# FNet mixing gated with a Mish MLP: the fifth block of columns takes its second row from the first row's partial and s3

## The chip, the cores and the metric

The kernel runs on one core of one Trainium2 chip. The core has TensorE (PE, matrix products), VectorE (DVE), ScalarE (ACT), GpSimd (POOL, hardly used here) and SyncE (SP), from which nearly all transfers between the chip's memory (HBM) and the on-chip memory are issued. PE adds its products up in PSUM, eight banks of 128 x 512 floats; DVE and ACT read the banks out. Each engine works off its own instructions in order and waits for the others by semaphores. The metric is the device time of one execution in microseconds (us); what counts is the median of several runs.

## The reference

```python
a = jnp.einsum("bsd,ed->bse", x, dft_hid_re)
b = jnp.einsum("bsd,ed->bse", x, dft_hid_im)
y = jnp.einsum("ts,bse->bte", dft_seq_re, a) - jnp.einsum("ts,bse->bte", dft_seq_im, b)
...
h = jnp.einsum("bsd,df->bsf", x, w1) + b1
act = h * jnp.tanh(softplus(h))          # Mish
mlp = jnp.einsum("bsf,fd->bsd", act, w2)
...
g = _sigmoid((x * gate_w).sum(-1, keepdims=True))
return g * y + (1 - g) * mlp
```

Here x is 2048 x 640 (s by d), the Fourier matrices are 2048 x 2048 and 640 x 640, w1 is 640 x 1728 and w2 1728 x 640, all in float32.

## The kernel before

**Products.** A float32 operand is split into a high and a low part (`split`, line 82): ACT copies it into a tile of the reduced type fp32r (line 80), DVE subtracts that from the original (line 77). A product of two split operands is three matmuls: high by high, high by low, low by high (`mm3`, line 91; all matmuls have line 89). Line 80 is thus every plain ACT copy and line 77 every DVE operation on two tensors.

**Stages.** The sequence transform comes first (four problems sq0 to sq3: real and imaginary matrix, two halves of the times each), then the hidden transform (hd0, hd1), then the first dense layer with Mish (written separately, `dense_rest` and `dense_first`), then the second dense layer (ou0, ou1). Between stages the results go through scratch buffers in HBM: u, y, act. The gate is worked out beside the sequence stage (`gate`, line 885: DVE sums, then two matmuls into a bank of their own, a sigmoid on ACT); g and 1 - g are kept in the buffers g and q. ou0 multiplies its results by q and adds y on the way out; ou1, called "early" in the code, has q already in its operands and adds y to intermediate results.

**A problem.** Each of the eight problems in the sequence, hidden and out stages is a product of 640 columns (five blocks of 128, the stationary operand) with two rows of 512 times, t1 and t2, over kh pairs of k (8, 5 and 6). The moving operands of a pair are a11 and a12 (t1, first and second half of k), a21 and a22 (t2). Four of the five blocks are multiplied with seven products for eight, in the manner of Strassen and Winograd, with sums s1 to s4 of the moving operands. The fifth block is multiplied plainly, into the banks d1 (row t1) and d2 (row t2). A problem is three functions:

- `first`: a11 by two blocks (bank pair a) and by the fifth block (d1);
- `second`: steps "22", "21", "s2" and "s1" for every k. "22" multiplies a22 into p4 and d2, "21" multiplies a21 into d2, "s2" into a, "s1" into b. With the last k of "21", d2 is finished and copied out (`done`), and the kept results are copied back into the banks c;
- `third`: steps "12" (banks c and d1), "s3" (a) and "s4" (b), with s3 = a11 - a21.

For sq1, sq2, hd1 and ou1 `first` runs well before `second`, and its results lie "aside" in HBM (three tiles, `part` 0 to 2); `a_ready` and the code after "21" load them back into banks (`preload`, line 281, an ACT copy into PSUM). In ou0 and ou1 `second` begins with a step `rest` (line 564) for the k that are left over, which opens its banks itself (the flag in its list of uses).

**Order.** Everything is emitted by one loop over the steps (line 1040), and each engine runs its instructions in the order in which this loop emits them. An iteration i first prepares the steps up to i + 7 (LEAD; 6 in the dense stage): sums and splits on DVE and ACT. Loads are issued 9 steps ahead of that, as long as enough of the 20 slots of the pool f are free. Then come the matmuls of step i, the stores that are due (three steps after the result), the step's `post` (reading banks out), the events that `at` registered for i, and then jobs (weights to be prepared, the gate) if an estimate of DVE's clock is behind PE's. PSUM banks and slots are handed out from lists, first freed first given. All loads and stores but one go through SP's queue in this order; one that has to wait for its slot or its value holds up those behind it.

Of the kernel before, what the change touches and what calls it, by code (L numbers as in the profile page):

```python
# [45 lines left out]
def fnet_mish_gate(ctx: ExitStack, tc: tile.TileContext, xn, xt, c_re, c_im, wd_re, wd_im,  # L46
# [134 lines left out]
    def b_sums(f, g):  # L181

        t = FS.get()
        tt(f[:, A2], f[:, B2], f[:, A2], OP.subtract)
        tt(f[:, B2], g[:, B2], f[:, B2], OP.subtract)
        tt(t[:, A2], g[:, B2], f[:, A2], OP.subtract)
        tt(t[:, B2], g[:, A2], t[:, A2], OP.subtract)
        return t
# [104 lines left out]
    class Problem:  # L293
# [8 lines left out]
        def first(self, new=False):  # L302
            st, kh = self.st, self.st.kh
            pa, pd = ("ax", "dx") if self.aside else ("a", "d1")
            for k in range(kh):
# [24 lines left out]
                def post():  # L330
                    if self.aside:
                        for dst, f in zip(self.aside, copy_out(pa) + copy_out(pd)):
                            store(dst, f, f)
                    else:
                        KEEP["p1"] = copy_out("a", True)
                if new:
                    raw += [(("xa", k), st.row(k)[:, A2])]
                if last:
                    takes[len(steps)] = 3 if self.aside else 2
# [3 lines left out]
        def second(self):  # L343
# [4 lines left out]
            def sums(k, raws):  # L348
                a22, a21, a11 = (RAW.pop(r[0]) for r in raws)
                s1 = FS.get()  # L350
                tt(s1, a21, a22, OP.add)
                tt(a11, s1, a11, OP.subtract)
                own.update({("22", k): a22, ("21", k): a21, ("s1", k): s1, ("s2", k): a11})
# [3 lines left out]
                "21": lambda k: [("d2", blocks(st.XA[k], 2 * P, 1))],  # L357
# [3 lines left out]
            opens = {("22", "p4"), ("22", "d2"), ("s1", "b")}  # L361
# [5 lines left out]
            def post(p, k):  # L367
# [4 lines left out]
                elif p == "21":  # L372
                    self.done("d2", 4, t2)
# [7 lines left out]
                    if self.aside:  # L381
                        d = [RAW.pop(("part", 2))]
                        if self.early:
                            y = YT.pop((4, t1))
                            tt(d[0], d[0], y, OP.add)
                            FS.put(y)
                        preload("d1", d)
                        FS.put(*d)
# [16 lines left out]
            if st.kind == "out":  # L405
                def e_post():
                    KEEP["r22"] = add_out("e", ys(t2, 2, 3)) if self.early else copy_out("e")
                if self.early:
                    self.y_load(n - 4, t2, 2, 3)
                rest(t2, [("e", 2, True), ("e", 3, True), ("p4", 0, True), ("p4", 1, True), ("d2", 4, True)], e_post)  # L410
            for p, k in in_turn(kh, ("22", "21", "s2", "s1"), ("22", "21", "s2", "s1"), ("22", "21", "s2", "s1")):
# [7 lines left out]
                def mms(p=p, k=k, key=key):  # L419
                    for name, b in uses[p](k):  # L420
                        product(name, b, key, k == 0 and (p, name) in opens and not (st.kind == "out" and name != "b"),
                                k == kh - 1)
                    op_done(key)
                    if self.end and (p, k) in ends:
                        W.put(st.XA[k])
                        if k == kh - 1:
                            W.put(*[w for w in st.XT2 if w])
                preps.append(lambda p=p, k=k, key=key: c_split(key, own.pop((p, k))))
                step(raw, preps, mms, lambda p=p, k=k: post(p, k))
                if k == kh - 1:  # L430
                    takes[i] = (p == "21" or p == "s1" and 2) if self.early else 1 if p == "21" else 2
                    if self.early and p != "s1":
                        takes[i - 4] = 2
                        if p == "21":
                            self.y_load(i - 4, t2, 4)
                            self.y_load(i - 4, t1, 0, 1, 4)
                        else:
                            self.y_load(i - 4, *{"22": (t2, 0, 1), "s2": (t1, 2, 3)}[p])
                if (p, k) == ("21", kh - 1):
                    done = i  # L440
            if self.out:
                for t in (t1, t2):
                    at(n - 2, lambda t=t: QT.update({t: fs_load(qsc[t])}))
                self.y_load(done - 5, t2, 4)
            ends = {("s1", k) for k in range(kh)}
            if self.aside:
                for j in range(3):
                        at(n - 6 if j < 2 else done - 6, lambda j=j: RAW.update({("part", j): fs_load(self.aside[j])}))
# [3 lines left out]
        def third(self, over=False):  # L452
# [3 lines left out]
            def sums(k, raws):  # L456
                a12, a11, a21, a22 = (RAW.pop(r[0]) for r in raws)
                tt(a11, a11, a21, OP.subtract)
                FS.put(a21)
                tt(a22, a22, a11, OP.subtract)  # L460
                tt(a22, a12, a22, OP.subtract)
                own.update({("12", k): a12, ("s3", k): a11, ("s4", k): a22})
# [3 lines left out]
                "s3": lambda k: [("a", blocks(st.XT13[k], 2 * P, 2))],  # L466
# [13 lines left out]
            def post(p, k):  # L480
# [4 lines left out]
                elif p == "s3":  # L485
# [4 lines left out]
                    free_banks("a")  # L490
                elif p == "12":
# [5 lines left out]
            for p, k in in_turn(kh, ("12", "s3", "s4"), ("12", "s3", "s4"), ("s3", "12", "s4")):  # L497
# [14 lines left out]
                def mms(p=p, k=k, key=key):  # L512
# [4 lines left out]
                    op_done(key)  # L517
                    if self.end and p == "s4":
                        W.put(st.XB[k], st.XT13[k])
                preps.append(lambda p=p, k=k, key=key: c_split(key, own.pop((p, k))))  # L520
                step(raw, preps, mms, lambda p=p, k=k: post(p, k))
                if k == kh - 1 and p != "s3":
                    takes[i] = 3 if p == "12" else 2
                if self.out and k == kh - 1:
                    self.y_load(i - (4 if p == "s3" else 2), *{"s3": (t2, 0, 1, 2, 3), "12": (t1, 0, 1, 4), "s4": (t1, 2, 3)}[p])
# [5 lines left out]
        def done(self, name, d, t):  # L531

            for j, ps in enumerate(PS.pop(name)):
# [4 lines left out]
                elif self.early and name == "d2":  # L538
                    y = YT.pop((d, t))
                    tt(f, ps, y, OP.add)  # L540
                    FS.put(y)
# [591 lines left out]
```

## Time and profile before

| | us |
|---|---|
| median of 3 runs | 886.82 |
| lowest, highest | 885.35, 889.29 |
| span of the profiled execution (what its own time is counted by) | 882.2 |
| PE busy | 864.0 (98%) |
| DVE busy | 724.2 (82%) |
| ACT busy | 477.5 (54%) |
| matmuls | 3780 |
| bytes moved | 217.32 MB |

The span of the profiled execution is from its first to its last instruction; a run's time is somewhat longer, since it holds what lies around them. Busy times are of each engine by itself, and they overlap. In the lists of waits a row names the engine, its line and the tile it writes, what it waited for, the total, the number and the longest. In the windows each engine has its busy time and its number of instructions, and PEclk is the clock that TensorE was granted, 1.00 being full. In the timeline a row is the start, the duration, the engine, the line, the operation and the tiles (written <- read), with the idle time just before it in brackets and what ended that.

### The profile page before, as it was taken

How to read it: one execution, taken by the hardware profiler on the slowest of the kernel's cores; microseconds unless marked ns; L12 is line 12 of the kernel's file. 1: busy time of each engine (PE TensorE's matmuls, PEld its weight loads, DVE VectorE, ACT ScalarE, POOL GpSimd, SP SyncE). 2: the span in 40 equal slices, each digit the busy share in tenths (PEclk: the TensorE clock that was granted, in tenths of full speed). 3: DMA queues.
4: the chain of work that ended last, by engine and by line, in shares of the span. 5: the costliest groups of instructions: out<-in, count | busy, mean ns of one | idle time of the engine just before them, and what ended most of it. 6: DMA issues, size and time to landing. Idle time of an engine off the chain costs nothing.

```text
span 882.2 us, 12203 instructions
## 1 busy us (share of the span) xinstructions
PE 864.0 (98%) x3780; PEld 710.4 (81%) x3780; DVE 724.2 (82%) x1262; ACT 477.5 (54%) x909; POOL 0.2 (0%) x4
## 2 busy tenths in 40 slices
PE   8999999999999999999999999899899999999998
PEld 6888888888888888888888888687688788888886
DVE  5999987899799668998997987663875889798994
ACT  6756545454565545647665667543644656442442
POOL 0000000000000000000000000000000000000000
PEclk9999999999999999999999999999999999999999
DMA  9975759596889664768767795489676777394952
GB/s 323 328 236 175 245 185 324 164 312 235 302 275 351 202 221 156 259 226 283 265 236 273 247 316 178 138 308 367 204 256 214 268 260 240 133 330 142 367 203 107
DMA packets 119392, 217.32 MB, mean 246 GB/s; under 512 B 13600, under 2 KB 16032, under 8 KB 119328
## 3 DMA queue, kind: packets, MB, share of 16 engines
q1 hardware_dynamic: 119184, 216.43, 71.6%
q8 instruction: 29, 0.48, 0.2%
q14 instruction: 35, 0.29, 0.1%
q10 hardware_dynamic: 144, 0.13, 0.0%
HBM read 170.11 MB, written 46.40 MB: 245 GB/s over the span
## 4 chain that ended last, share of the span: by engine, by line
PE 93%; DVE 3%; ACT 1%; DMA 1%; issue 1%; SPq 0%; DVEq 0%; ACTq 0%
PE ps L89 93%; DVE f L77 1%; DVE wl L77 1%; ACT wh L80 1%; DMA y<-f 1%; DVE rl L77 0%; DMA f<-in_xn_dram 0%; ACT f L671 0%; DMA act<-f 0%; DVE fx L77 0%; ACT f L80 0%; ACT rh L80 0%; SPq L1031 0%; SPq L1051 0%; DVE f L477 0%
## 5 line engine op out<-in xcount | busy, mean ns | idle before, releaser
L89 PE MATMUL ps<-rh,wh 128*128 128x512 f32 x1067 | 415.7, 390 | 7.4 <-ACT f L80 3.4
L89 PE MATMUL ps<-rh,wl 128*128 128x512 f32 x1053 | 409.4, 389 | 0.0
L89 PE MATMUL ps<-rl,wh 128*128 128x512 f32 x1052 | 409.1, 389 | 0.0
L80 ACT ACTIVATE rh<-f 128x512 fp32r<-128x512 f32 x413 | 243.7, 624 | 158.3 <-DVE f L77 103.9
L77 DVE TENSOR_TENSOR rl<-f,rh 128x512 fp32r<-128x512 f32 x411 | 267.0, 685 | 47.7 <-ACT rh L80 47.0
L89 PEld LDWEIGHTS ps<-rh,wh 128*128 128x128 f32 x1067 | 200.4, 188 | 52.7 <-ACT f L80 5.0
L89 PEld LDWEIGHTS ps<-rh,wl 128*128 128x128 f32 x1053 | 197.7, 188 | 40.9
L89 PEld LDWEIGHTS ps<-rl,wh 128*128 128x128 f32 x1052 | 197.4, 188 | 40.9 <-DVE rl L77 0.2
L77 DVE TENSOR_TENSOR f<-f,f 128x512 f32<-128x512 f32 x303 | 207.0, 689 | 19.2 <-DMA u<-f 6.3
L80 ACT ACTIVATE f<-ps 128x512 f32<-128x512 f32 (+1 forms) x146 | 84.9, 593 | 92.7 <-PE ps L89 74.7
L80 ACT ACTIVATE wh<-f 128x512 fp32r<-128x512 f32 (+2 forms) x158 | 68.9, 475 | 49.4 <-DVE f L77 40.4
L77 DVE TENSOR_TENSOR f<-ps,f 128x512 f32<-128x512 f32 x90 | 59.0, 685 | 35.1 <-PE ps L89 35.1
L77 DVE TENSOR_TENSOR wl<-f,wh 128x512 fp32r<-128x512 f32 (+2 forms) x157 | 73.8, 502 | 16.2 <-ACT wh L80 16.0
L89 PE MATMUL ps<-wh,wh 128*128 128x512 f32 x201 | 79.3, 395 | 5.4 <-ACT f L80 2.8
L89 PE MATMUL ps<-wl,wh 128*128 128x512 f32 x196 | 77.0, 393 | 0.0
L89 PE MATMUL ps<-wh,wl 128*128 128x512 f32 x195 | 76.6, 393 | 0.0
L77 DVE TENSOR_TENSOR wl<-fx,wh 128x640 fp32r<-128x640 f32 (+3 forms) x82 | 43.7, 554 | 11.6 <-ACT wh L80 11.6
L671 ACT ACTIVATE f<-f,b1s 128x512 f32<-128x512 f32 x36 | 25.9, 721 | 49.2 <-DVE f L77 49.2
L89 PEld LDWEIGHTS ps<-wh,wh 128*128 128x128 f32 x201 | 38.0, 189 | 15.4 <-ACT f L80 4.2
L80 ACT ACTIVATE wh<-fx 128x128 fp32r<-128x128 f32 (+5 forms) x83 | 40.6, 514 | 10.5 <-DMA fx<-in_xn_dram 3.5
L89 PEld LDWEIGHTS ps<-wh,wl 128*128 128x128 f32 x195 | 37.0, 190 | 7.8
L89 PEld LDWEIGHTS ps<-wl,wh 128*128 128x128 f32 x196 | 37.1, 189 | 7.5
(43 smaller groups left out, 177.3 us busy)
## 6 DMA issues: line engine op xcount, KB each, us to landing
f<-in_c_re_dram SPq DMA_DIRECT2D x128, 256.0 KB, 4.2
f<-in_c_im_dram SPq DMA_DIRECT2D x128, 256.0 KB, 4.1
f<-act SPq DMA_DIRECT2D x84, 256.0 KB, 5.2
f<-u SPq DMA_DIRECT2D x80, 256.0 KB, 4.6
f<-in_xt_dram SPq DMA_DIRECT2D x64, 256.0 KB, 4.6
act<-f SPq DMA_DIRECT2D x54, 256.0 KB, 4.5
u<-f SPq DMA_DIRECT2D x40, 256.0 KB, 3.5
y<-f SPq DMA_DIRECT2D x40, 256.0 KB, 4.5
```

The costliest lines, as they stand in the source:

```text
L77: nc.vector.tensor_tensor(o, a, b, op=op)
L80: nc.scalar.activation(o, a, AF.Copy, scale=scale)
L89: nc.tensor.matmul(ps, a, b, start=start, stop=stop, skip_group_check=True)
L671: nc.scalar.activation(o[rows], src[rows], AF.Mish, bias=b1s[rows, f:f + 1])
```

## The change

Row t2 of the fifth block is a21 X1 + a22 X2, where X1 and X2 are the fifth block's stationary parts. Before, both products are made in `second`. After, a21 is written as a11 + s3 with s3 = a21 - a11: the product of a11 with X1 is d1's partial from `first`, s3 X1 is made in `third` in the step "s3", and a22 X2 stays in `second`. So:

- the steps "21" are gone; a21 is not split, and s1 is formed in its slot (one slot of f less). Steps in all: 540 before, 486 after;
- d2 begins with the kept partial. In a problem with its `first` just before, the partial is copied out of d1 and into d2 at the end of `first`; in the others the event `d_ready`, one step before `second` begins, copies it from its tile (in ou1 with y added before on DVE);
- d2 stays open to the end of the last "s3" of `third` and is read out there; all eight banks are then in use in `third`;
- the preloads of c and d1 move from "21" to "22", and the loads of y move with the steps;
- s3 and the stationary sum that goes with it change sign.

DVE operations on two tensors: 1231 before, 1177 after; ACT activations: 907 before, 866 after; matmuls and transfers are as many as before (3780, 829).

```diff
--- before.py
+++ after.py
@@ -182,7 +182,7 @@
 
         t = FS.get()
         tt(f[:, A2], f[:, B2], f[:, A2], OP.subtract)
-        tt(f[:, B2], g[:, B2], f[:, B2], OP.subtract)
+        tt(f[:, B2], f[:, B2], g[:, B2], OP.subtract)
         tt(t[:, A2], g[:, B2], f[:, A2], OP.subtract)
         tt(t[:, B2], g[:, A2], t[:, A2], OP.subtract)
         return t
@@ -332,11 +332,13 @@
                         for dst, f in zip(self.aside, copy_out(pa) + copy_out(pd)):
                             store(dst, f, f)
                     else:
-                        KEEP["p1"] = copy_out("a", True)
+                        KEEP["p1"], KEEP["d"] = copy_out("a", True), copy_out("d1", True)
+                        preload("d2", KEEP["d"])
+                        FS.put(*KEEP.pop("d"))
                 if new:
                     raw += [(("xa", k), st.row(k)[:, A2])]
                 if last:
-                    takes[len(steps)] = 3 if self.aside else 2
+                    takes[len(steps)] = 3
                 step(raw, [prep], mms, post if last else None)
 
 
@@ -347,18 +349,26 @@
 
             def sums(k, raws):
                 a22, a21, a11 = (RAW.pop(r[0]) for r in raws)
-                s1 = FS.get()
-                tt(s1, a21, a22, OP.add)
-                tt(a11, s1, a11, OP.subtract)
-                own.update({("22", k): a22, ("21", k): a21, ("s1", k): s1, ("s2", k): a11})
+                tt(a21, a21, a22, OP.add)
+                tt(a11, a21, a11, OP.subtract)
+                own.update({("22", k): a22, ("s1", k): a21, ("s2", k): a11})
 
             uses = {
                 "22": lambda k: [("p4", blocks(st.XA[k], 3 * P, 2)), ("d2", blocks(st.XB[k], 4 * P, 1))],
-                "21": lambda k: [("d2", blocks(st.XA[k], 2 * P, 1))],
                 "s2": lambda k: [("a", [part(st.XT13[k], 4 * P, 5 * P), t2_part(st, k)])],
                 "s1": lambda k: [("b", blocks(st.XT13[k], 0, 2))],
             }
-            opens = {("22", "p4"), ("22", "d2"), ("s1", "b")}
+            opens = {("22", "p4"), ("s1", "b")}
+
+            def d_ready():
+                d = KEEP["d"] = RAW.pop(("part", 2))
+                if self.early:
+                    y = YT.pop((4, t2))
+                    tt(y, y, d, OP.add)
+                    preload("d2", [y])
+                    FS.put(y)
+                else:
+                    preload("d2", [d])
 
             def a_ready():
                 KEEP["p1"] = [RAW.pop(("part", j)) for j in range(2)]
@@ -369,8 +379,6 @@
                     return
                 if p == "22":
                     KEEP["p4"] = add_out("p4", ys(t2, 0, 1)) if self.early else copy_out("p4")
-                elif p == "21":
-                    self.done("d2", 4, t2)
                     c = KEEP.pop("p1")
                     if self.early:
                         for a, y in zip(c, ys(t1, 0, 1)):
@@ -379,13 +387,13 @@
                     preload("c", c)
                     FS.put(*c)
                     if self.aside:
-                        d = [RAW.pop(("part", 2))]
+                        d = KEEP.pop("d")
                         if self.early:
                             y = YT.pop((4, t1))
-                            tt(d[0], d[0], y, OP.add)
+                            tt(d, d, y, OP.add)
                             FS.put(y)
-                        preload("d1", d)
-                        FS.put(*d)
+                        preload("d1", [d])
+                        FS.put(d)
                 elif p == "s2":
                     KEEP["u2"] = add_out("a", ys(t1, 2, 3), True) if self.early else copy_out("a", True)
                 else:
@@ -407,8 +415,8 @@
                     KEEP["r22"] = add_out("e", ys(t2, 2, 3)) if self.early else copy_out("e")
                 if self.early:
                     self.y_load(n - 4, t2, 2, 3)
-                rest(t2, [("e", 2, True), ("e", 3, True), ("p4", 0, True), ("p4", 1, True), ("d2", 4, True)], e_post)
-            for p, k in in_turn(kh, ("22", "21", "s2", "s1"), ("22", "21", "s2", "s1"), ("22", "21", "s2", "s1")):
+                rest(t2, [("e", 2, True), ("e", 3, True), ("p4", 0, True), ("p4", 1, True), ("d2", 4, False)], e_post)
+            for p, k in in_turn(kh, ("22", "s2", "s1"), ("22", "s2", "s1"), ("22", "s2", "s1")):
                 i, key = len(steps), ("c", st.kind, len(steps))
                 raw, preps = [], []
                 if p == "22":
@@ -421,31 +429,28 @@
                         product(name, b, key, k == 0 and (p, name) in opens and not (st.kind == "out" and name != "b"),
                                 k == kh - 1)
                     op_done(key)
-                    if self.end and (p, k) in ends:
-                        W.put(st.XA[k])
-                        if k == kh - 1:
-                            W.put(*[w for w in st.XT2 if w])
+                    if self.end and p == "s2" and k == kh - 1:
+                        W.put(*[w for w in st.XT2 if w])
                 preps.append(lambda p=p, k=k, key=key: c_split(key, own.pop((p, k))))
                 step(raw, preps, mms, lambda p=p, k=k: post(p, k))
                 if k == kh - 1:
-                    takes[i] = (p == "21" or p == "s1" and 2) if self.early else 1 if p == "21" else 2
+                    takes[i] = (p == "s1" and 2) if self.early else 2
                     if self.early and p != "s1":
                         takes[i - 4] = 2
-                        if p == "21":
-                            self.y_load(i - 4, t2, 4)
+                        if p == "22":
+                            self.y_load(i - 4, t2, 0, 1)
                             self.y_load(i - 4, t1, 0, 1, 4)
                         else:
-                            self.y_load(i - 4, *{"22": (t2, 0, 1), "s2": (t1, 2, 3)}[p])
-                if (p, k) == ("21", kh - 1):
-                    done = i
+                            self.y_load(i - 4, t1, 2, 3)
             if self.out:
                 for t in (t1, t2):
                     at(n - 2, lambda t=t: QT.update({t: fs_load(qsc[t])}))
-                self.y_load(done - 5, t2, 4)
-            ends = {("s1", k) for k in range(kh)}
             if self.aside:
                 for j in range(3):
-                        at(n - 6 if j < 2 else done - 6, lambda j=j: RAW.update({("part", j): fs_load(self.aside[j])}))
+                    at(n - 6, lambda j=j: RAW.update({("part", j): fs_load(self.aside[j])}))
+                if self.early:
+                    self.y_load(n - 6, t2, 4)
+                at(n - 1, d_ready)
                 at(n, a_ready)
 
 
@@ -455,15 +460,15 @@
 
             def sums(k, raws):
                 a12, a11, a21, a22 = (RAW.pop(r[0]) for r in raws)
-                tt(a11, a11, a21, OP.subtract)
-                FS.put(a21)
-                tt(a22, a22, a11, OP.subtract)
+                tt(a21, a21, a11, OP.subtract)
+                FS.put(a11)
+                tt(a22, a22, a21, OP.add)
                 tt(a22, a12, a22, OP.subtract)
-                own.update({("12", k): a12, ("s3", k): a11, ("s4", k): a22})
+                own.update({("12", k): a12, ("s3", k): a21, ("s4", k): a22})
 
             uses = {
                 "12": lambda k: [("c", blocks(st.XB[k], 0, 2)), ("d1", blocks(st.XB[k], 4 * P, 1))],
-                "s3": lambda k: [("a", blocks(st.XT13[k], 2 * P, 2))],
+                "s3": lambda k: [("a", blocks(st.XT13[k], 2 * P, 2)), ("d2", blocks(st.XA[k], 2 * P, 1))],
                 "s4": lambda k: [("b", blocks(st.XB[k], 2 * P, 2))],
             }
 
@@ -488,6 +493,7 @@
                             tt(o, ps, o, OP.add)
                             self.give(name + i, t2, o)
                     free_banks("a")
+                    self.done("d2", 4, t2)
                 elif p == "12":
                     self.done("c", 0, t1)
                     self.done("d1", 4, t1)
@@ -515,14 +521,16 @@
                     for name, b in uses[p](k):
                         product(name, b, key, False, k == kh - 1)
                     op_done(key)
+                    if self.end and p == "s3":
+                        W.put(st.XA[k])
                     if self.end and p == "s4":
                         W.put(st.XB[k], st.XT13[k])
                 preps.append(lambda p=p, k=k, key=key: c_split(key, own.pop((p, k))))
                 step(raw, preps, mms, lambda p=p, k=k: post(p, k))
-                if k == kh - 1 and p != "s3":
-                    takes[i] = 3 if p == "12" else 2
+                if k == kh - 1:
+                    takes[i] = {"12": 3, "s3": 1, "s4": 2}[p]
                 if self.out and k == kh - 1:
-                    self.y_load(i - (4 if p == "s3" else 2), *{"s3": (t2, 0, 1, 2, 3), "12": (t1, 0, 1, 4), "s4": (t1, 2, 3)}[p])
+                    self.y_load(i - (4 if p == "s3" else 2), *{"s3": (t2, 0, 1, 2, 3, 4), "12": (t1, 0, 1, 4), "s4": (t1, 2, 3)}[p])
                     if p == "s4":
                         at(i, lambda: FS.put(QT.pop(t1), QT.pop(t2)))
                 if st.kind == "out" and (p, k) == ("s4", 1):
@@ -535,10 +543,6 @@
                 if self.out:
                     tt(f, ps, QT[t], OP.mult)
                     self.add_y(d + j, t, f)
-                elif self.early and name == "d2":
-                    y = YT.pop((d, t))
-                    tt(f, ps, y, OP.add)
-                    FS.put(y)
                 else:
                     copy(f, ps)
                 psum.put(ps)
```

## The prediction

> **What bounds the kernel now.** I read the page's busy times first, then the chain that ended last in order of time, then the waits of PE, and last the stretches in which those waits lie.
>
> ```profile
> span 882.2 us, 12203 instructions
> PE 864.0 (98%) x3780; PEld 710.4 (81%) x3780; DVE 724.2 (82%) x1262; ACT 477.5 (54%) x909; POOL 0.2 (0%) x4
> L80 ACT ACTIVATE rh<-f 128x512 fp32r<-128x512 f32 x413 | 243.7, 624 | 158.3 <-DVE f L77 103.9
> L77 DVE TENSOR_TENSOR rl<-f,rh 128x512 fp32r<-128x512 f32 x411 | 267.0, 685 | 47.7 <-ACT rh L80 47.0
> L80 ACT ACTIVATE f<-ps 128x512 f32<-128x512 f32 (+1 forms) x146 | 84.9, 593 | 92.7 <-PE ps L89 74.7
> ```
> ```profile
> 7.40 547.11 PE ps L89 x2412
> ...
> 706.29 172.16 PE ps L89 x757
> ```
> ```profile
> PE ps L89 <- ACT f L80: 6.2, 5, 2.4
> PE ps L89 <- DVE f L77: 4.6, 4, 1.4
> ```
> ```profile
> 616.00:638.00 22.00, 17.17 (x65) 12.98 (x66) 17.47 (x28) 15.39 (x28) 0.00 (x0) 0.92 0.62 211
> 792.00:814.00 22.00, 22.00 (x99) 18.22 (x98) 18.53 (x29) 3.68 (x7) 0.00 (x0) 1.00 0.42 136
> 814.00:836.00 22.00, 22.00 (x99) 18.22 (x98) 21.37 (x36) 11.15 (x21) 0.00 (x0) 1.00 1.02 365
> ```
>
> The reader is to see that PE is the bound nearly everywhere: 547.11 us for 2412 matmuls without a break (0.2268 us each) over the sequence and hidden stages, and again 172.16 us for 757 in the out stage. The windows there show 22.00 of 22 for PE, though DVE reaches 21.37 in one of them. PE waits only between these two stretches (554.5 to 706.3, the dense stage) and at the start. The number of matmuls does not change (3780), so time can come or go only through PE's waits. The profiled execution has a span of 882.2; the median of the runs, 886.82, lies 4.6 above it, and I keep that 4.6.
>
> **The change, part by part.** *Splits.* a21 is no longer split, once per k in each problem: 4x8 (sequence stage), 2x5 (hidden) and 2x6 (out) = 54 splits. That takes 54 x 0.685 = 37.0 us from DVE and 54 x 0.624 = 33.7 us from ACT; 13 more PSUM copies on ACT (kept partials out, preloads in, less the former d2 copies) give back 13 x 0.593 = 7.7. Outside the dense stage this is worth 0: the cover is PE itself, at 22.00 of 22. There is no split in the dense stage to save. The sums stay as many, only their signs turn, and the 829 transfers stay as many; one slot of the f pool less is needed in second.
>
> *Matmuls.* The three per k that multiplied a21 move from second to the steps "s3" of third, where s3 replaces a21. Same number, same rate: 0. But the bank d2 stays open until s3's end, it has to be preloaded before second's first use, and its way out lies behind s3. I follow that at each place where a problem hands over to the next.
>
> *Handing over from ou0 to ou1 (out stage).* These rows of before are DVE's and PE's.
>
> ```profile
> 798.20 0.69 DVE L77 TENSOR_TENSOR f<-ps,f 128x512 f32<-128x512 f32 x1 [3.02 <-PE ps L89]
> ...
> 804.37 0.68 DVE L77 TENSOR_TENSOR f<-ps,f 128x512 f32<-128x512 f32 x1
> 805.08 1.42 DVE L77 TENSOR_TENSOR f<-f,f 128x512 f32<-128x512 f32 x2
> 806.42 1.28 DVE L77 TENSOR_TENSOR wl<-f,wh 128x512 fp32r<-128x512 f32 x2
> 807.62 0.69 DVE L77 TENSOR_TENSOR fx<-ps,f 128x512 f32<-128x512 f32 x1
> ...
> 808.95 0.68 DVE L77 TENSOR_TENSOR f<-ps,f 128x512 f32<-128x512 f32 x1
> ...
> 811.61 1.29 DVE L77 TENSOR_TENSOR rl<-fx,rh 128x512 fp32r<-128x512 f32 x2
> 812.81 0.68 DVE L77 TENSOR_TENSOR f<-ps,f 128x512 f32<-128x512 f32 x1
> ```
> ```profile
> 805.48 0.39 PE L89 MATMUL ps<-rh,wh 128*128 128x512 f32 x1
> ...
> 811.00 0.60 ACT L80 ACTIVATE ps<-fx 128x512 f32<-128x512 f32 x1 [12.79 <-DVE f L77]
> ```
>
> DVE works off third's results in order: four groups of three for s3 (6.17 us for three of them, 798.20 to 804.37, so 2.05 each), two splits (1.20, 806.42 to 807.62), three pairs for c and d1 (3.99, 807.62 to 811.61), two splits (1.20), two pairs for b. It is 9 us behind PE already, which nobody waits for. After the change the new event d_ready of ou1 stands behind all of that: y + partial on DVE, then the preload of d2 on ACT, and the step "rest" with which ou1 begins needs it for its last five matmuls. Start: s3's first bank is ready three matmuls earlier (d2's three come behind), at 798.20 - 0.68 = 797.52. Then 4 x 2.05 + one new pair for d2 of 1.33 (807.62 to 808.95) = 807.07; splits 808.27; c and d1 812.26; splits 813.46; two pairs 816.12; the add 0.69, 816.81; the preload 0.60, about 817.45. PE begins "rest" at 805.48 (that row) as before. Its 11th matmul (807.75) takes a bank of c, which DVE reads from 808.27 to 808.96: a wait of 1.25. Its 16th takes c's second, read until 810.29: 0.15. So it comes to d2 at 811.5 and waits until 817.45, 5.95. Together **+7.4**. In before this step opened its d2 bank itself and had no such wait. Next late after it is nothing: DVE has done the splits of six steps ahead. Bounds: 5 (DVE's pairs at their closest pitch) and 9.
>
> A wait of 6 us also has a price after it. Rows from the dense stage:
>
> ```profile
> 620.82 0.39 PE L89 MATMUL ps<-rh,wl 128*128 128x512 f32 x1
> 623.61 0.58 PE L89 MATMUL ps<-wh,wh 128*128 128x512 f32 x1 [2.39 <-ACT f L80]
> ...
> 626.97 0.55 PE L89 MATMUL ps<-wh,wl 128*128 128x512 f32 x1
> 627.36 0.40 PE L89 MATMUL ps<-rh,wh 128*128 128x512 f32 x1
> ```
>
> After an idle time of 2.39 us, nine matmuls took 3.75 us (623.61 to 627.36) where nine at full clock take 2.04; the window 616 to 638 has a granted clock of 0.92. So **+1.7** after a gap of 6, with 0 and 3.4 (twice that) as ends. The Trainium skill, "TensorE: Matmul & The Clock Gate", Part 1, has the clock fall to half after an idle window of about 3.4 us, the windows running freely; if the whole window had to be idle, an estimate by that page is that a gap of 6 us holds one in three cases of four, and the sum without it would be 1.7 lower. The row above, with a gap of 2.4, says that less suffices, and I go by the row.
>
> *Handing over from sq0 to sq1.* The steps are fewer (no "21"), so seven steps of lead reach further: the third "22" of sq1 is now prepared in the step before sq1 begins, ahead of the copies out of b and of d2's preload in ACT's queue, and its split waits for a load.
>
> ```profile
> 130.84 2.56 DVE L77 TENSOR_TENSOR f<-ps,f 128x512 f32<-128x512 f32 x4 [2.00 <-PE ps L89]
> ```
> ```profile
> 134.04 1.41 SPq L1051 DMA_DIRECT2D f<-in_c_im_dram  x3
> 139.34 1.11 ACT L80 ACTIVATE ps<-f 128x512 f32<-128x512 f32 x2
> ```
> ```profile
> f<-in_c_im_dram SPq DMA_DIRECT2D x128, 256.0 KB, 4.1
> ```
>
> On SP's queue this load stands behind the stores of s3's results. In before the first load behind them was issued 3.2 us after the first add (130.84 to 134.04). After the change one more store and three loads of the gate stand ahead, at some 0.47 a piece (1.41 for three) 1.9 more; the adds begin 1.1 before s3's end: issued 4.0, landed 4.1 later, 8.1 after s3's end. ACT then does the split, two copies and the preload, pitch 0.55 (1.11 for two): ready 10.4 after s3's end. PE wants d2 36 matmuls after s3's end, at 8.2. **+2.2**; ends 0 (the load comes in time, as it does now) and 4.1 (a whole landing later). In sq2, hd1 and sq3 the operands are there earlier: 0.
>
> *The gate's matmuls.* In third now all eight banks are taken (a, b, c two each, d1, d2). Gate 1 and gate 3 come right behind "s3" and get the bank that its third add frees. Adds follow at 0.64 (2.56 for four above); the third begins about 0.2 after s3's end and ends at 0.9, so PE waits 0.95 each time: **+1.9** for both. Ends 0 and 6 (DVE late by 2). That a bank held longer takes away cover is also what the Trainium skill says, "Perfetto Trace Analysis", Matmuls: independent groups should rotate through different banks, so that reading one out lies beside the next; no run here shows yet what it costs.
>
> *Dense stage.* The slots of f come round in another order. In before ACT's copy out of a bank waits for a slot whose y store is still under way:
>
> ```profile
> 616.09 0.60 ACT L80 ACTIVATE f<-ps 128x512 f32<-128x512 f32 x1 [4.62 <-DMA y<-f]
> 617.85 0.69 DVE L77 TENSOR_TENSOR rl<-f,rh 128x512 fp32r<-128x512 f32 x1 [6.54 <-ACT rh L80]
> 619.06 5.40 DVE L77 TENSOR_TENSOR f<-f,f 128x512 f32<-128x512 f32 x8
> ```
>
> After the change this copy gets another slot, and the chain of eight sums behind it, on which the waits from 616 to 630 hang, begins up to 2.7 us earlier. How much of it PE sees depends on whether its idle time gathers in one longer gap and brings the half clock with it: between 0 and -4.3 (2.6 and the 1.7 of the clock), I take **-1.7**. The other waits (565 to 573, 692, 706) keep their place: the jobs with which they go come at the same matmuls.
>
> Sum: 7.4 + 1.7 + 2.2 + 1.9 - 1.7 = +11.5; span 893.7, with 4.6 around it **898.3 us**.
>
> **The rivals.** *Faster.* The dense stage alone decides: the window 616 to 638 shows PE busy for 17.17 of 22, so 4.8 us idle, and the half clock costs 1.7; if all of it goes with the y store and ou1's wait is hidden, the time is 886.8 - 6.5 = 880.3. For it speaks the row of 4.62; against it that DVE's order in ou0 is fixed by the code. It would decide if d_ready's add were done by 811, that is if DVE were 6 us less behind than its rows show. 0.09.
> *Hardly a change.* The wait in ou1 is there, but the half clock after it, sq1 and the gates cost nothing and the dense stage gives its 4.3: 7.4 - 4.3 = +3.1, 890. For it: loads landed in time everywhere in before. 0.14.
> *Much slower.* DVE is late at the gates (2.5 to 3 us each) and sq1's load a landing later, dense gives nothing: 7.4 + 3.4 + 4.1 + 5.5 = +20, 907. 0.10.
> The forecast, with its terms between their ends, has 0.67.
>
> **How the numbers follow.** 0.5% is 4.4 us, about what a measurement of this kernel can tell from no change. Slower by more than that are the forecast and the fourth case, 0.67 + 0.10; the third (+3.1) lies within it, the first below. The range, 887 to 904, takes in the third case and ends short of the fourth; the first and the fourth, 0.19, are left out. Faster 0.09, same 0.14, slower 0.77.
>
> **What would show it.** PE should have one long gap at the start of ou1, about 6 us, ended by ACT's preload of one bank, followed by some nine matmuls at 0.43 us; two waits of about 1 us ahead of the gate's matmuls; one of 2 us in sq1's first steps; and fewer or shorter waits between 616 and 630. ACT's and DVE's busy times should fall by about 26 and 37 us without any gain from it. If the gap in ou1 is under 2 us, the forecast is wrong in its largest term; if dense loses its waits altogether, in its sign.

## The result, and the profile after

The changed kernel takes 900.12 us (median of 4 runs, 898.9 to 900.73) against 887.87 us for the kernel before in the same comparison (885.35 to 889.29). The ratio is 1.0142, with a 95% interval of 1.0122 to 1.0162: slower by 1.4%, 12.25 us between the medians, where the prediction had +11.5 and 898.3 us.

First the page of the changed kernel, its span and busy times, and then the first four rows of its list of PE's waits (total, number, longest).

```profile
span 897.1 us, 12029 instructions
PE 869.1 (97%) x3780; PEld 711.2 (79%) x3780; DVE 694.4 (77%) x1208; ACT 457.8 (51%) x868; POOL 0.2 (0%) x4
```
```profile
PE ps L89 <- DVE f L77: 10.0, 7, 2.8
PE ps L89 <- ACT ps L80: 7.9, 3, 5.7
PE ps L89 <- ACT rh L80: 2.5, 1, 2.5
PE ps L89 <- ACT f L80: 1.8, 2, 1.3
```

DVE is busy 29.8 us less than before and ACT 19.7 us less, and the kernel is slower. "ACT ps", the wait for a preload into a bank, was not among PE's waits before; now it has three entries. In the timeline these are PE's rows where a problem begins (sq1, sq2, ou1) and where a gate's matmuls follow s3 (stationary operand "ones"). The bracket is the idle time just before the matmul and what ended it. A "slow matmul" is one after which the next starts 0.43 us later and not 0.23.

```profile
143.54 0.50 PE L89 MATMUL ps<-rh,wh 128*128 128x512 f32 x1 [1.84 <-ACT ps L80]
...
218.62 0.50 PE L89 MATMUL ps<-rh,ones 128*128 128x512 f32 x1 [0.70 <-DVE f L77]
230.72 0.50 PE L89 MATMUL ps<-rh,wh 128*128 128x512 f32 x1 [0.36 <-ACT ps L80]
...
302.91 0.50 PE L89 MATMUL ps<-rh,ones 128*128 128x512 f32 x1 [0.70 <-DVE f L77]
...
814.06 0.50 PE L89 MATMUL ps<-rh,wh 128*128 128x512 f32 x1 [1.08 <-DVE f L77]
822.53 0.79 PE L89 MATMUL ps<-rh,wh 128*128 128x512 f32 x1 [5.72 <-ACT ps L80]
823.12 0.63 PE L89 MATMUL ps<-rl,wh 128*128 128x512 f32 x1
823.55 0.63 PE L89 MATMUL ps<-rh,wl 128*128 128x512 f32 x1
```

At sq1 the other side is in ACT's timeline: a split that waits 2.62 us for its load, two copies out of b, and behind them the copy of d2's start value into its bank.

```profile
141.40 0.63 ACT L80 ACTIVATE rh<-f 128x512 fp32r<-128x512 f32 x1 [2.62 <-DMA f<-in_c_im_dram]
141.94 1.06 ACT L80 ACTIVATE f<-ps 128x512 f32<-128x512 f32 x2
142.89 0.60 ACT L80 ACTIVATE ps<-f 128x512 f32<-128x512 f32 x1
```

The other side of the largest wait, at ou1, in the changed kernel's timeline of DVE and ACT. DVE starts on s3's results at 802.57 and works through them without a pause; the last thing in its queue is the pair at 820.55 (an add for b, then y + partial for d2), and only then can ACT copy d2's start value into its bank.

```profile
802.57 0.69 DVE L77 TENSOR_TENSOR f<-ps,f 128x512 f32<-128x512 f32 x1 [6.43 <-PE ps L89]
...
820.55 1.29 DVE L77 TENSOR_TENSOR f<-f,f 128x512 f32<-128x512 f32 x2
```
```profile
821.88 0.60 ACT L80 ACTIVATE ps<-f 128x512 f32<-128x512 f32 x1 [21.34 <-DVE f L77]
```

PE issues the same number of matmuls in both kernels and does almost everything in the same order of problems. So the start of the n-th matmul in the one trace can be set against that in the other; where the difference jumps, time was lost or won. The two spans differ by 14.94 us, and this is how they come apart:

| place | forecast | from the two traces |
|---|---|---|
| first 20 matmuls (load of x, first steps of the clock) | 0 | +2.05 |
| entry to sq1 | +2.2 | +2.31 |
| gates 1 and 3, behind s3 | +1.9 | +1.97 |
| entry to sq2 | 0 | +0.76 |
| three smaller places (sq3 0.29, hd1 0.10, ou0's first 0.43) | 0 | +0.82 |
| dense stage, 554 to 640 | -1.7 | -2.96 |
| entry to ou1, waits | +7.4 | +8.02 |
| entry to ou1, slow matmuls behind the gap | +1.7 | +2.05 |
| the rest | 0 | -0.08 |
| sum | +11.5 | +14.94 |

The first row isn't the change's. Two kernels whose first instructions are those of before (the one without the split of a21 and the one with a slot swapped, below) started the matmul after the first 20 at 12.38 and 12.39 us, the changed one at 12.33, the two profiles of before at 10.28 and 10.54, and others up to 13.71. The granted clock goes with it: it is full from 6.07 and 6.03 us on in the two profiles of before, and in the other nine for good only from between 11.19 and 14.04 us. Without this row 12.9 remain, against 12.25 between the medians.

### The profile page after: what moved, and what is told of

It is laid out like the page before. It is cut to its first block, busy times and chain, and to the rows that moved or that the text cites. A ratio compares the mean times of both kernels' runs of the same rounds, so it can differ in the third digit from the quotient of the medians.

```text
span 897.1 us, 12029 instructions
## 1 busy us (share of the span) xinstructions
PE 869.1 (97%) x3780; PEld 711.2 (79%) x3780; DVE 694.4 (77%) x1208; ACT 457.8 (51%) x868; POOL 0.2 (0%) x4
## 4 chain that ended last, share of the span: by engine, by line
PE 88%; DVE 6%; ACT 2%; DMA 2%; issue 1%; SPq 0%; DVEq 0%; ACTq 0%
PE ps L89 88%; DVE f L77 4%; DVE rl L77 1%; DVE wl L77 1%; ACT wh L80 1%; DMA act<-f 1%; ACT f L80 1%; DMA f<-in_xn_dram 0%; ACT f L675 0%; ACT rh L80 0%; DMA f<-in_c_re_dram 0%; DMA f<-in_c_im_dram 0%; DVE fx L77 0%; ACT ps L80 0%; SPq L1035 0%
## 5 line engine op out<-in xcount | busy, mean ns | idle before, releaser
L89 PE MATMUL ps<-rh,wl 128*128 128x512 f32 x1037 | 404.7, 391 | 0.0
L80 ACT ACTIVATE rh<-f 128x512 fp32r<-128x512 f32 x366 | 218.4, 625 | 168.0 <-DVE f L77 103.9
L77 DVE TENSOR_TENSOR rl<-f,rh 128x512 fp32r<-128x512 f32 x365 | 240.9, 686 | 63.1 <-ACT rh L80 62.2
L80 ACT ACTIVATE f<-ps 128x512 f32<-128x512 f32 (+2 forms) x151 | 87.5, 593 | 109.4 <-PE ps L89 98.8
L77 DVE TENSOR_TENSOR wl<-f,wh 128x512 fp32r<-128x512 f32 (+2 forms) x152 | 70.5, 496 | 22.8 <-ACT wh L80 22.7
L89 PE MATMUL ps<-wh,wh 128*128 128x512 f32 x216 | 84.6, 391 | 0.6 <-ACT f L80 0.5
L89 PE MATMUL ps<-wh,wl 128*128 128x512 f32 x211 | 82.4, 390 | 0.0
L89 PEld LDWEIGHTS ps<-wh,wh 128*128 128x128 f32 x216 | 40.7, 188 | 10.1 <-ACT f L80 1.6
L89 PEld LDWEIGHTS ps<-wh,wl 128*128 128x128 f32 x211 | 39.7, 188 | 8.4
```

Of the source, the lines that this page charges most:

```text
L77: nc.vector.tensor_tensor(o, a, b, op=op)
L80: nc.scalar.activation(o, a, AF.Copy, scale=scale)
L89: nc.tensor.matmul(ps, a, b, start=start, stop=stop, skip_group_check=True)
```

## The experiments

**y added at d2's way out.** If DVE's queue is what holds d2 back at ou1, then the add must leave that queue.

```diff
 def d_ready():
     d = KEEP["d"] = RAW.pop(("part", 2))
-    if self.early:
-        y = YT.pop((4, t2))
-        tt(y, y, d, OP.add)
-        preload("d2", [y])
-        FS.put(y)
-    else:
-        preload("d2", [d])
+    preload("d2", [d])
...
 # done(), after s3:
+    elif self.early and name == "d2":
+        y = YT.pop((d, t))
+        tt(f, ps, y, OP.add)
+        FS.put(y)
```

> The changed kernel, but ou1's d_ready copies the bare partial into the bank d2 by ACT, and y is added on DVE when d2 is read out at the end of ou1's s3. My theory (the 6.12 us gap at 822.53 is the add y + partial standing at the end of DVE's queue behind ou0's results, and the matmuls at 0.43 us behind it are its consequence): the gap of 6.1 goes, the half clock (2.05 us) goes with it, the wait of 1.5 us on the bank of c a little before it stays; time about 8.5 us less, 891.6. Rival (ACT or the bank, not DVE's queue, makes d2 late): the gap stays above 4 us and the time above 897.

896.05 us (ratio to before 1.0105, 1.0081 to 1.0129), 4.1 less than the changed kernel. The gap of 6.12 us from matmul to matmul is gone and so are the slow matmuls behind it: the trace is 6.45 + 2.05 us earlier at that point. The wait on c's bank stays (1.48 us between two matmuls, at 815.00). So the mechanism holds, but the time is not the 891.6 that was expected: 4.4 us are lost again 32 us later. The rows of this kernel's PE, ACT and DVE there:

```profile
849.95 0.74 PE L89 MATMUL ps<-rh,wh 128*128 128x512 f32 x1 [2.51 <-ACT ps L80]
850.50 0.63 PE L89 MATMUL ps<-rl,wh 128*128 128x512 f32 x1
```
```profile
849.30 1.80 ACT L80 ACTIVATE ps<-f 128x512 f32<-128x512 f32 x3 [10.48 <-DVE f L77]
```
```profile
843.91 0.69 DVE L77 TENSOR_TENSOR f<-f,f 128x512 f32<-128x512 f32 x1 [4.38 <-DMA f<-act]
```

The preload of c at the end of "22" stands behind sums on DVE that wait for a load of act. In the changed kernel the same preload runs at 850.26, about as late, but PE comes there 7.6 us later, held up by the gap and the slow matmuls, and doesn't notice. One wait had covered another. The kernel with all remedies, below, takes these sums out of the way.

**The gate's bank after 12.**

```diff
-        while not psum.free:
+        while len(psum.free) < (4 if t % 2 else 1):
             yield 1
```

> The changed kernel, but gates 1 and 3 may take a bank only when at least four are free, which is after the step 12 of third and no longer right behind s3. My theory (PE waits for the third DVE add of s3's results before each of the gate's matmuls): the waits of 1.0 us before the matmuls of gates 1 and 3 go, 2.0 us together, time about 898.1. Rival (the gate waits for its own operand's split, which the jobs bring late): the two waits stay, wherever the gate stands, and the time is 900.

899.08 us, ratio 1.0142 (1.0118 to 1.0167): no difference that the times could tell. The trace tells more. Both waits at the gates are gone (0.98 and 0.99 us). A later gate would have helped a late operand too, but in the changed kernel the operand was there: DVE's last split ahead of gate 1 ended at 215.28, 3.3 us before the matmul at 218.62, and what ended that wait was the third of DVE's four adds that begin at 216.60. So the waits were for the bank. But the gate's work moved on by some steps and the entry to sq2 got worse by 1.34 us:

```profile
223.36 0.39 PE L89 MATMUL ps<-rh,ones 128*128 128x512 f32 x1
...
232.58 0.50 PE L89 MATMUL ps<-rh,wh 128*128 128x512 f32 x1 [1.71 <-ACT ps L80]
```

**A shorter lead at sq1's entry.** Step 78 is sq1's third "22".

```diff
-  while ready < n_all and ready <= i + (LEAD_D if ready in narrow else LEAD):
+  while ready < n_all and ready <= i + (LEAD_D if ready in narrow or ready == 78 else LEAD):
```

> The changed kernel, but the third step 22 of sq1 is prepared with a lead of six steps in place of seven, so that ACT's copies out of b and the preload of d2 come before its split. My theory (ACT stands at that split and waits for its load): the wait of 2.1 us at PE's entry to sq1 (143.54) goes, time about 897.8. Rival (the kept partial itself is loaded too late): the wait stays.

899.04 us, 1.0138 (1.0111 to 1.0165). In the trace the wait on d2 at 143.54 is gone (-2.03), but 12 matmuls later PE waits for the other preload, that of a, which is an event of the next step:

```profile
147.19 0.50 PE L89 MATMUL ps<-rh,wh 128*128 128x512 f32 x1 [1.38 <-ACT ps L80]
```

ACT's rows show two splits ahead of that preload: the same one as before at 143.68, which now waits 0.94 us for its load, and that of the step behind it, which waits for a sum on DVE. That sum had waited 3.79 us for its own load.

```profile
146.02 0.63 ACT L80 ACTIVATE rh<-f 128x512 fp32r<-128x512 f32 x1 [1.71 <-DVE f L77]
146.55 1.10 ACT L80 ACTIVATE ps<-f 128x512 f32<-128x512 f32 x2
```

So the place in ACT's queue is what counts, as the theory had it, and one step wasn't enough. The next run takes one more step off, in sq1 and in sq2 (step 126). Steps are prepared in order, so the step behind each is held back with it:

```diff
+  ... ready <= i + (5 if ready in (78, 126) else LEAD_D if ready in narrow else LEAD):
```

> The changed kernel with a lead of five steps for the third step 22 of sq1 and of sq2, so that the preloads of d2 and of a both come before its split in ACT's queue (with six only d2's did, and the wait went to a). My theory: the waits at PE's entry to sq1 (2.2) and to sq2 (0.76) go, time about 897.2. Rival (the load itself is late, and PE then waits for the split of that step): a wait of 1.5 us or more appears at the matmuls of that step.

896.75 us, 1.0109 (1.0087 to 1.013), 3.4 less than the changed kernel. In the trace 2.19 us came back at sq1 and 0.65 at sq2, and no wait took their place at the step whose split is now later. The loads were never too late for PE; they were too late for what had been queued behind the splits.

**The relief alone.** What is the saved split worth by itself? This kernel leaves out the split of a21 and multiplies a22 in its place, so its results are those of another product; it serves for the time alone.

```diff
 # before: the step "21" takes the split parts that "22" has made
+ if p == "21":
+     return FS.put(own.pop((p, k)))
  c_split(key, own.pop((p, k)))
+ if p == "22":
+     OPS["21", id(self), k] = OPS[key]
```

> The kernel before, with the steps 21 kept, but their operand is not split: they multiply with the split parts of a22, so that the results are those of another product (the split of a21 is left out, 54 on ACT and 54 on DVE). It has the relief of ACT and DVE alone, with no d2 held open. My theory (the relief lies beside PE): PE stays at full rate outside the dense stage and the time is within 2 us of before, 886 to 889, in the dense stage up to 3 us either way by the order of jobs. Rival (the relief is what took 2.7 us from the waits between 616 and 630): PE's waits there get shorter by 2 to 3 us as in the changed kernel.

886.07 us in 12 runs, ratio 0.9993 (0.9977 to 1.0009). The two windows show why, at the same place in both kernels (columns after the window's length: busy PE, weight loads, DVE, ACT; further on the granted clock). First the kernel before, then the one without the split:

```profile
330.00:352.00 22.00, 22.00 (x99) 18.23 (x98) 18.50 (x35) 12.95 (x26) 0.00 (x0) 1.00 0.48 158
```
```profile
330.00:352.00 22.00, 22.00 (x99) 18.23 (x98) 17.15 (x34) 10.25 (x23) 0.00 (x0) 1.00 0.63 204
```

DVE and ACT do less; PE was at 22.00 of 22 and is so still. In the dense stage PE's waits from 616 to 630 did not get shorter in that trace: the relief isn't what won time there.

**The slot in the dense stage.** One line in the kernel before gives the slot with the pending y store to a load.

```diff
+ if i == 384:
+     FS.free.insert(2, FS.free.pop(0))
```

> The kernel before with one change: at step 384 of the dense stage the first free slot of f, whose y store is under way, is given to the second load and not to ACT's copy out of the bank. My theory (the wait of ACT for that store sets the waits of PE from 616 to 630): ACT's copy at 616.09 starts 2 to 2.7 us earlier, PE's waits there get 2 to 2.7 us shorter, time 884 to 886. Rival (the chain of eight sums on DVE sets them, whenever it may begin): PE's waits from 616 to 630 stay within 0.5 us in sum.

885.82 us in 10 runs, ratio 0.9989 (0.9975 to 1.0003): at most a quarter of a percent, and not told from nothing. ACT's copy no longer waits for the store: counted from the same matmuls it starts 2.7 us earlier. PE's gap at 616.74 (1.71 us from matmul to matmul) is gone, but the waits from 616 to 630 lose only about 1 us in sum, where 2 to 2.7 were expected. What is left looks like the changed kernel's dense stage and no longer like that of before. ACT's and PE's rows of the kernel with the slot swapped, then PE's rows of the changed kernel:

```profile
615.65 0.60 ACT L80 ACTIVATE f<-ps 128x512 f32<-128x512 f32 x1 [1.95 <-PE ps L89]
```
```profile
620.35 0.50 PE L89 MATMUL ps<-rh,wh 128*128 128x512 f32 x1 [1.34 <-ACT f L80]
623.16 0.50 PE L89 MATMUL ps<-wh,wh 128*128 128x512 f32 x1 [0.46 <-ACT f L80]
629.68 0.50 PE L89 MATMUL ps<-wh,wh 128*128 128x512 f32 x1 [2.80 <-DVE f L77]
```
```profile
625.32 0.50 PE L89 MATMUL ps<-rh,wh 128*128 128x512 f32 x1 [1.29 <-ACT f L80]
628.19 0.50 PE L89 MATMUL ps<-wh,wh 128*128 128x512 f32 x1 [0.53 <-ACT f L80]
634.71 0.50 PE L89 MATMUL ps<-rh,wh 128*128 128x512 f32 x1 [2.81 <-DVE f L77]
```

Three waits, the same sizes and the same releasers. So the slot's order is what changed the waits there. In before four waits between 616 and 630 were together 6.05 us over the normal spacing, in the changed kernel three are 5.11. Of the rest of the -2.96 about 1.6 is the clock: in the changed kernel's trace no slow matmuls follow that stage's gaps, in the trace with the swapped slot eight do, in before's nine. That part isn't the change's; where it comes from is shown under "The half clock". About 0.4 us lies further ahead: the waits of before at 564.99 and 567.79 (1.62 and 0.44 us) are gone, and that at 572.88 has grown from 1.37 to 2.70 (579.99 in the changed kernel). All seven traces of the changed kernel and its variants have this; no run tells which part of the change brings it.

**The kernel before again.**

> The kernel before once more, unchanged, for its trace. If the 2.05 us by which PE's first 20 matmuls were later after the change are no part of it (first load and the clock's first steps), this start scatters by 1 to 2 us between executions of one kernel too; if they belong to the change, the 20th matmul starts at 10.3 us again, as in the first profile of before. The waits from 616 to 630 should be as before but for the half clock, which may or may not follow the gap of 2.8.

884.42 us (span 882.0). Gaps and slow matmuls are those of the first profile to within 0.3 us, and the matmul after the first 20 started at 10.54. So this run alone would not have shown that the start scatters; the kernels with before's start at 12.38 and 12.39 do.

**All remedies together**, with two more: in ou1's first step d2 is multiplied before p4, and the step whose sums stood ahead of c's preload (468) has a lead of five.

```diff
- rest(t2, [("e", 2, True), ("e", 3, True), ("p4", 0, True), ("p4", 1, True), ("d2", 4, False)], e_post)
+ use = [("e", 2, True), ("e", 3, True), ("p4", 0, True), ("p4", 1, True)]
+ use.insert(2 if self.early else 4, ("d2", 4, False))
+ rest(t2, use, e_post)
...
+ ... ready <= i + (5 if ready in (78, 126, 468) else LEAD_D if ready in narrow else LEAD):
```

> The changed kernel with all the remedies: y added at d2's way out; in ou1's first step d2 is multiplied before p4, so that the banks of c are wanted 1.1 us later; the gates 1 and 3 take their bank after 12; a lead of five for the third 22 of sq1 and sq2 and, in ou1, for the step whose sums stood ahead of the preload of c (the new wait of 2.9 us in the kernel with y added at the end). My theory: PE's waits that the change brought are gone, which is 8.0 + 2.0 + 2.0 + 2.3 + 0.8 less than the changed kernel, time about 885, within 2 us of before. Rival (lighter DVE and ACT are still worth something, once the waits are away): below 882. Rival (each wait has another behind it): above 890.

886.77 us in 13 runs, against 886.76 for the kernel before in the same comparison; the ratio is 0.9995 (0.998 to 1.0009). PE's waits in its profile:

```profile
PE ps L89 <- DVE f L77: 7.5, 4, 2.8
PE ps L89 <- ACT rh L80: 3.1, 1, 3.1
PE ps L89 <- ACT f L80: 2.2, 3, 1.0
PE ps L89 <- DVE rh L944: 1.6, 1, 1.6
PE ps L89 <- DVE rl L77: 0.9, 1, 0.9
PE ps L89 <- ACT ps L80: 0.6, 1, 0.6
```

The waits for a preload are down from 7.9 us to 0.6, and the kernel is where it was before the change. The profiled execution happened to be the longest of the 13 (892.38 us): it has slow matmuls at the start and behind two gaps of the dense stage.

> The kernel with all remedies but that for the gates, which take their bank right behind s3 as in the changed kernel. My theory: the two waits of 1.0 us before the gate's matmuls are back (+2.0), and the wait of 1.3 us in sq2 (at 235.19), which came with the later gate, is gone, so that it is within 1 us of the kernel with all remedies, 886 to 888. Rival (the wait at 235.19 comes from the lead of five): it stays, and the time is 889.

888.35 us in 12 runs, ratio 1.0025 (1.001 to 1.004). In the trace the gates' waits are back (0.98 each) and the gap of 1.31 us from matmul to matmul at 235.19 is gone, which thus came with the later gate and not with the lead. That would make 0.7 us between the two kernels. Their ratios differ by 0.3%, 2.7 us, and the intervals only just don't meet (1.0009 and 1.001), so the later gate seems to be worth a little more than these two places show; where the rest lies isn't settled.

## Why the prediction was right

*What bounds the kernel, and the splits at 0.* Right, and shown: with the relief alone the ratio is 0.9993, with an interval of 0.0016 either way.

*ou1.* Right step by step. The prediction had the last add begin at 816.12 and the preload done at 817.45 on before's time; at that point the changed kernel was 5.05 us late already, so 821.2 and 822.5. Measured: 821.2 (the second of the pair at 820.55) and 822.48. The waits on c's banks were put at 1.25 and 0.15 and came to 1.24 and 0.07; that on d2 at 5.95, measured 5.89. The remaining 0.8 of the 8.02 are the longer spacings just behind each wait and the first two slow matmuls.

*"Next late after it is nothing."* Wrong, and without effect on the time, because the delay itself covered it. It only showed when the delay was taken away: the preload of c in "22" was late by 2.9 us.

*sq1 and the gates.* Right in place, cause and size (2.31 for 2.2, and 0.98 and 0.99 for 0.95). That the preload of a would be next was not said.

*Busy times.* They were to fall by about 37 us on DVE and 26 on ACT; they fell by 29.8 and 19.7. The counts are as forecast (54 operations less on DVE, 41 on ACT). The prediction multiplied them by mean durations, but the records of neighbours overlap, and busy time counts an overlap once: in the prediction's row of 413 splits 413 x 0.624 makes 257.7, and their busy time is 243.7. Nothing hangs on it, since this time lies beside PE.

*"In sq2, hd1 and sq3 the operands are there earlier: 0."* Too low: 0.76 at sq2, where d2's preload was in time and that of a stood behind the split of the next step, which waited for a sum on DVE and with it for a load (ACT's rows below), and 0.29 at sq3, where the copy out of d1 and the preload of d2 follow each other in ACT's queue.

```profile
229.54 0.63 ACT L80 ACTIVATE rh<-f 128x512 fp32r<-128x512 f32 x1 [2.24 <-DVE f L77]
230.08 1.10 ACT L80 ACTIVATE ps<-f 128x512 f32<-128x512 f32 x2
```

*The dense stage.* The mechanism was right: the slot alone, swapped in the kernel before, brings about the same three waits. What it is worth without the clock is 0.9 us in these traces, not 1.7. That the waits from 565 to 573 keep their place was wrong: two are gone and the third is twice as long.

*The half clock.* Right that the gap of 6 us is followed by it; 2.05 for 1.7, eleven slow matmuls for nine. The reason given was too simple: it took the row of 2.4 us as proof that such a gap suffices. The same gap in the dense stage (between 3.06 and 3.09 us from matmul to matmul, always before the same matmul) stands in seven traces of the changed kernel and its variants. In four of them full speed goes on, in three the clock drops with the next few matmuls. The changed kernel first, then the one with a lead of six:

```profile
579.99 0.50 PE L89 MATMUL ps<-rh,wh 128*128 128x512 f32 x1 [2.70 <-DVE f L77]
580.32 0.40 PE L89 MATMUL ps<-rl,wh 128*128 128x512 f32 x1
```
```profile
580.61 0.79 PE L89 MATMUL ps<-rh,wh 128*128 128x512 f32 x1 [2.68 <-DVE f L77]
581.20 0.63 PE L89 MATMUL ps<-rl,wh 128*128 128x512 f32 x1
```

The idle time is the same within 0.02 us, so its length alone doesn't decide. What does can be read from the granted clock. In every trace it changes only on a grid of 3.41 us, which lies elsewhere in each execution: in before it is half from 623.88 to 627.30, in the changed kernel from 821.07 to 827.90, which is two such windows. Here are the windows at the gap, in the same two kernels. A row has the stretch, its length, PE's busy time and matmuls, the granted clock, and last the DMA's share and GB/s.

```profile
575.30:578.72 3.42, 1.98 (x9) 1.00 0.99 369
578.72:582.13 3.41, 2.15 (x9) 1.00 0.68 239
```
```profile
577.24:580.65 3.41, 0.73 (x5) 1.00 1.05 401
580.65:584.06 3.41, 3.41 (x8) 0.50 0.33 115
```

In the changed kernel a window's edge cuts the gap into 1.44 and 1.26 us of idle time, and full speed stays; with the lead of six all 2.68 us lie in one window, and the next has half the clock. That fits the free-running window of the Trainium skill, "TensorE: Matmul & The Clock Gate", Part 1, better than the prediction's reading of one row. But the window need not be idle from end to end, as an idle window on that page of the Trainium skill would be: 1.94 us of idle time in one were enough (last section). The gap at ou1 (5.7 us idle) is longer than a window; in each of the four traces that have it (the changed kernel and those with the later gate and the leads of six and five) one window lies wholly inside it and half the clock follows.

The wait of 2.8 us at 634.71 is another such case: in the changed kernel an edge at 633.34 cuts it into 1.43 and 1.37, and no slow matmul follows; in the kernel with the slot swapped 2.66 us of it lie in one window, and eight follow.

*The sum.* That +11.5 comes so near to the 12.25 between the medians is in part luck. Without the start the trace has 12.9. The places put at nothing or too low make 2.65 more than forecast (0.11 at sq1, 0.07 at the gates, 0.76 at sq2, 0.82 at the three smaller places, 0.62 and 0.35 at ou1, less 0.08), and the dense stage takes 1.26 off that, because of a clock that is not the change's.

## What to carry to other kernels

A saved operation on an engine that nobody waits for was worth nothing here, and what was done to save it had to be paid for: a bank that stays open longer and a start value that has to be there earlier. When such a value is made on an engine that works in order, count what stands ahead of it in that queue at that moment; an engine that is 9 us behind without harm becomes the bound as soon as one new thing at the end of its queue is wanted. Before a delay is called the only one at its place, look for what it covers: the next late preload showed only when the first was gone.

## What the runs showed of the hardware that I had not expected

Whether a wait costs the clock goes by the 3.41 us window in which it lies. In the eleven traces, behind the first 25 us, the profile has some 2750 windows that began at full clock and were followed by another one before the kernel's end. Fifteen of them were followed by half the clock, and in these PE was idle for 1.94 to 3.41 us; in all the others it was idle for 1.78 at most. (PE's busy time is modelled in part, so the limit is known only to be near these two numbers.) The smallest that lost the clock, in the kernel with all remedies but the gate's, and the largest that kept it, in the one with a lead of five, each with the window behind it:

```profile
620.64:624.05 3.41, 1.47 (x7) 1.00 0.84 299
624.05:627.46 3.41, 3.41 (x9) 0.50 0.33 121
```
```profile
622.68:626.09 3.41, 1.63 (x7) 1.00 0.68 260
626.09:629.50 3.41, 3.41 (x16) 1.00 0.66 193
```

What is left to chance is where the grid lies in an execution. For the gap of 3.1 us it decided between nothing and 1.7 to 3.0 us, as much as some of the waits under study.

The matmul after the first 20 starts anywhere from 10.28 to 13.71 us in eleven traces, and kernels that begin alike differ by 2 us. Effects of a microsecond in this kernel are therefore read from where two traces part, and not from the difference of two spans.
